# Decay attention then a two-layer block: own places for the first four jobs' inputs, and their transfers in program order

## The chip, the cores and the metric

The kernel runs on one core of a Trainium2 chip. Five engines work side by side, each through its own list of instructions in a fixed order: TensorE (PE in the profile, its weight loads PEld), VectorE (DVE), ScalarE (ACT), GpSimd (POOL) and SyncE (SP), which here only issues transfers. The metric is the device time of one launch in microseconds; lower is better. What is shown as a time is the median of three runs.

## The reference

For 8 batches and 8 heads, with a sequence S of 576 and head size 64, attention with a decay is computed: the scores are `q k^T / 8`, to which the difference of two running sums of `log(clip(f))` is added, with a causal mask, a softmax over the row, and the product with `v`. The result is laid out as 4608 tokens of 512 features, and goes through `g(x @ w_in) @ w_out` with a hidden size of 2048:

```python
cum = np.cumsum(np.log(np.clip(f, 0.0001, 1.0)), axis=-1)
scores = scale * np.matmul(q, k.transpose(0, 1, 3, 2)) + cum[..., :, None] - cum[..., None, :]
attn = softmax(where(causal, -1e9, scores))        # divided by (sum + 1e-9)
x = np.matmul(attn, v)                              # then to (tokens, heads * head size)
h = x @ w_in
g = where(h >= 1, h, where(h <= -1, 0, (h + 1) ** 2 / 4))
out = g @ w_out
```

The two weights come as 64-bit floats, so each block of a weight is 1 MB to be loaded, and has to be split into two 16-bit parts on the chip. `q`, `k`, `v` and `f` are 32-bit floats.

## The kernel before, in words

**Jobs.** Attention is done in jobs, each one pair of heads of one batch. Batch 0 is cut in two by rows of the score matrix: jobs 0 to 3 are its four head pairs for the first 256 rows, jobs 4 to 7 the same pairs for rows 256 to 575; from job 8 on a job is a head pair with all 576 rows. A job's rows are taken in blocks of 128. For a block PE makes the scores (L482); POOL makes the decay part from a broadcast row of sums, `ck`, and masks it (L488, L492); DVE adds both and finds the row's extreme (L571); ACT takes the exponential with its sum (L575). For the first five jobs ACT then makes a diagonal of the reciprocal sums (L502), PE turns the block with it (L513, L519), ACT copies it out (L524), and PE multiplies it with `v` (L544), from where ACT and DVE write the two 16-bit parts of `x` (L551, L552). Later jobs go another way (L589, L595, a transfer that transposes, L615).

**Inputs.** `load` (L330) brings `q` and `k` of a job into one of two buffers, `qk32`, by the job's parity; `early_prepare` (L375) turns them with PE (L388) and copies them out (L389). `load_decay` (L359) brings one head's decay row into one of three `ck` buffers, broadcast to all partitions; the sums themselves, `cum_d`, are written to memory by `decay_sums` (L150). `split_values` (L427) brings `v` of a job. `value_load` (L243) brings all of batch 0's `v` once more, in four parts, for its largest value (L256), from which a scale follows.

**Weights.** There are sixteen blocks, n = 0 to 15, of 1 MB each: an even n from `w_in`, an odd one from `w_out`. `weight_load` (L195) brings a block to a raw place: most lie in places of the result that are filled later, some in a buffer of `x` (table `RAW`). A place can be loaded again only when its last block was converted. `weight_split` converts two blocks at a time, here called a pair of blocks: DVE rearranges bits (L211, L214, L217), ACT sums squares (L221), PE and DVE make a scale (L131 to L140), ACT writes the high part (L225), POOL (L227, L228) and DVE (L230) the low one. `CONVERT` says how many pairs are done at each job, `LOADS` and `AHEAD` how far the loads may run ahead.

**The second part.** A unit of it is 256 tokens by 256 hidden features: PE (L657), ACT (L666, L667), DVE (L668), ACT (L670), DVE (L671), PE (L685). Units are put between the blocks of attention as soon as tokens and weights are there; those of `EARLY` begin with the first four pairs of weight blocks and the first 512 tokens.

**What sets the order.** The program is written as one sequence; a scheduler then gives each engine its list, moving instructions by its own estimate of when they can start. `in_order` pins an instruction: pinned instructions keep the order of the program. On the chip each engine goes strictly through its list. All transfers are issued by SP; each also waits until the one eight places ahead of it has landed. Before the change, the loads are not pinned.

## Time and profile before

| what | us |
|---|---|
| median of three runs (1118.39, 1119.46, 1121.65) | 1119.46 |
| the profiled execution | 1118.56 |
| its span | 1116.8 |
| PE busy in the span | 1017.8 |
| DVE busy in the span | 799.0 |
| ACT busy in the span | 790.0 |
| POOL busy in the span | 427.4 |

The span is the stretch from the first to the last instruction of the profiled execution; 1.8 us of its time lie outside. Times below count from the start of the span. In a row of the timeline stand the start, the time it took, the engine, the line, what is written from what, and how often; in brackets, how long the engine had been idle and what released it. "SPq" is the issue of a transfer, not its landing. A transfer's landing stands in the view of transfers, as a median from its issue. Line numbers are those of the kernel before; in the changed kernel the same code has other numbers (L153 became L158, L163 L172, L201 L210, L250 L265 or L267, L351 L362 or L378, L355 L382, L362 L389 or L399, L388 L428 or L433, L440 L480 or L499, L442 L501, L482 L541, L513 L572, L544 L603).

### The profile page before, as it was taken

The numbers are of one execution on the slowest core, as the hardware profiler recorded it, in microseconds if no ns is written. First come the engines' busy times: TensorE is split into PE (matmuls) and PEld (weight loads), VectorE is DVE, ScalarE is ACT, GpSimd is POOL, SyncE is SP. The second block draws the span as 40 slices with busy tenths as digits, with TensorE's granted clock in tenths as the row PEclk, the third lists the DMA queues.
The fourth block names the chain that finished last, engine by engine and source line by source line (L and its number), as shares of the span: only waits on it lengthen the run. The fifth ranks groups of instructions, "written<-read, shape, count | busy, mean of one in ns | idle before, by whom it ended". The sixth has DMA issues, their size and how long they took to land. (4 is left out here: it accounts for less than half of the span.)

```text
span 1116.8 us, 24410 instructions
## 1 busy us (share of the span) xinstructions
PE 1017.8 (91%) x8811; PEld 663.8 (59%) x8811; DVE 799.0 (72%) x2095; ACT 790.0 (71%) x1638; POOL 427.4 (38%) x679
## 2 busy tenths in 40 slices
PE   4647789667999999999999999999999999999998
PEld 3424455335566666666766666566666666677665
DVE  4785987887989888887667668888888787322222
ACT  3665887756877887788667768787878887444443
POOL 3486665634544543343223324344343442000000
PEclk9968889778999999999999999999999999999999
DMA  7957765575978657766653666775776462200000
GB/s 235 303 143 222 167 147 125 142 191 116 190 172 166 159 143 170 167 152 148 118 140 78 155 119 153 168 174 139 166 167 155 116 124 73 66 21 1 19 20 19
DMA packets 408281, 152.18 MB, mean 136 GB/s; under 512 B 383968, under 2 KB 384992, under 8 KB 408160
## 3 DMA queue, kind: packets, MB, share of 16 engines
q1 hardware_dynamic: 408160, 150.63, 57.6%
q8 instruction: 69, 1.13, 0.4%
q14 instruction: 52, 0.43, 0.1%
HBM read 75.64 MB, written 9.58 MB: 76 GB/s over the span
## 5 line engine op out<-in xcount | busy, mean ns | idle before, releaser
L657 PE MATMUL ph<-x,place 128*128 128x256 f16 (+3 forms) x4608 | 413.3, 248 | 6.4 <-DVE u L668 5.5
L685 PE MATMUL po<-place,g 128*128 128x512 f16 x1728 | 401.9, 382 | 12.4 <-ACT g L670 8.2
L657 PEld LDWEIGHTS <-place 128*128 128x128 f16 x4608 | 354.1, 99 | 66.3 <-issue 18.0
L685 PEld LDWEIGHTS <-g 128*128 128x128 f16 x1728 | 166.4, 99 | 192.0 <-ACT g L670 10.5
L488 POOL TENSOR_SCALAR sdr<-ck,nsig,cqs 128x128 f32<-128x128 f32 (+1 forms) x192 | 145.8, 763 | 149.2 <-DVE pr L595 137.3
L575 ACT ACTIVATE sdr<-sdr,nm 128x384 f32<-128x384 f32 (+1 forms) x248 | 137.4, 554 | 66.9 <-DVE nm L571 57.0
L668 DVE SCALAR_TENSOR_TENSOR u<-ph,z,u 128x512 f32<-128x512 f32 x128 | 95.8, 748 | 113.1 <-ACT u L667 112.5
L488 POOL TENSOR_SCALAR sd<-ck,nsig,cqs 64x576 f32<-64x576 f32 x48 | 60.0, 1250 | 248.7 <-ACT qs L414 109.3
L666 ACT ACTIVATE u<-ph,z 128x512 f32<-128x512 f32 x128 | 97.9, 765 | 78.4 <-PE ph L657 78.4
L482 PE MATMUL s<-qkT 64*64 64x512 f16 (+11 forms) x1056 | 119.6, 342 | 34.1 <-DVE nm L571 30.6
L595 DVE SCALAR_TENSOR_TENSOR pr<-sdr,rc,pr 128x384 f16<-128x384 f32 (+2 forms) x232 | 130.5, 596 | 21.6 <-ACT pr L589 20.4
L670 ACT ACTIVATE g<-u,z 128x512 f16<-128x512 f32 x128 | 91.9, 718 | 67.6 <-DVE u L668 67.3
L671 DVE SCALAR_TENSOR_TENSOR g<-u,z,g 128x512 f16<-128x512 f32 x128 | 96.7, 756 | 47.2 <-ACT g L670 46.5
L589 ACT ACTIVATE pr<-sdr,rc 128x384 f16<-128x384 f32 (+1 forms) x236 | 119.3, 556 | 12.1 <-DVE rc L586 5.3
L571 DVE CUSTOM_DVE_ANT_0 sdr<-s,sdr,nalpha 128x128 f32<-128x128 f32 (+1 forms) x192 | 99.0, 545 | 13.1 <-PE s L482 8.3
L492 POOL TENSOR_SCALAR_AFFINE_SELECT sdr<-sdr 128x128 f32<-128x128 f32 x248 | 93.9, 389 | 9.7
L667 ACT ACTIVATE u<-u 128x512 f32<-128x512 f32 x144 | 89.5, 622 | 2.0
L615 PE MATMUL s<-pT,vs 128*64 128x320 f16 (+3 forms) x1098 | 70.9, 282 | 4.7 <-DVE nm L571 4.7
L615 PEld LDWEIGHTS <-vs 128*64 128x64 f16 x1098 | 49.7, 112 | 27.3 <-issue 8.8
L488 POOL TENSOR_SCALAR sdr<-ck,cq 128x384 f32<-128x384 f32 (+3 forms) x56 | 39.9, 712 | 66.2 <-DVE pr L595 38.3
L482 PEld LDWEIGHTS <-qkT 64*128 64x128 f16 (+1 forms) x864 | 33.8, 99 | 51.3 <-issue 35.9
L414 ACT ACTIVATE qs<-qk,sc 128x640 f16<-128x640 f32 x48 | 37.0, 818 | 22.4 <-DVE sc L140 22.4
(154 smaller groups left out, 1013.8 us busy)
## 6 DMA issues: line engine op xcount, KB each, us to landing
ck<-cum_d SPq DMA_DIRECT2D x64, 288.0 KB, 3.8
out_dram<-ot SPq DMA_DIRECT2D x36, 256.0 KB, 2.1
qk<-in_k_dram SPq DMA_DIRECT2D x64, 128.0 KB, 2.7
vst<-in_v_dram SPq DMA_DIRECT2D x28, 288.0 KB, 3.3
v<-in_v_dram SPq DMA_DIRECT2D x62, 128.0 KB, 2.6
qk<-in_q_dram SPq DMA_DIRECT2D x56, 128.0 KB, 2.7
place<-in_moe_w_in_dram SPq DMA_DIRECT2D x6, 1024.0 KB, 7.2
place<-in_moe_w_out_dram SPq DMA_DIRECT2D x5, 1024.0 KB, 7.2
```

The lines of the kernel that those rows point to most:

```text
L482: nc.tensor.matmul(sds[h % len(sds)][1][p0:p1, c0:c1], lhsT=a[rows, q0 - w.s0:q0 - w.s0 + p1 - p0], rhs=b[rows, c0:c1], start=(i == 0), st ...
L488: nc.gpsimd.tensor_scalar(out=sd[p0:p1, 0:wid], in0=w.ck[h][p0:p1, 0:wid], scalar1=w.nsig if w.p < NQK else w.nsig[p0:p1], scalar2=w.cqs[p ...
L571: nc.vector.tensor_tensor_reduce(out=a, in0=sp[:, 0:wid], in1=a, scale=w.nalpha, scalar=BIG, op0=ALU.add, op1=ALU.min, accum_out=nm[:, i:i ...
L575: nc.scalar.activation(a, a, AF.Exp, bias=nm[:, i:i + 1], scale=-1.0, accum_out=sm[:, i:i + 1])
L589: nc.scalar.activation(pr[:, :, 0, i, :], a, AF.Copy, scale=rc[:, i:i + 1])
L595: nc.vector.scalar_tensor_tensor(out=pr[:, :, 1, i, :], in0=a, scalar=rc[:, i:i + 1], in1=pr[:, :, 0, i, :], op0=ALU.mult, op1=ALU.subtract,)
L615: nc.tensor.matmul(av[64 * h:64 * h + 64, at + s0:at + s1], lhsT=w.vs[:, vl, h, t, :], rhs=w.pT[:, t, pl, h, s0:s1], start=(t == 0 and pi ...
L657: nc.tensor.matmul(ph[:, fi, a0:a1], lhsT=wi[fb][:, wl, t, fi * P:(fi + 1) * P], rhs=xs[b][:, t, xl, s0:s0 + a1 - a0], start=(fi == 0 and ...
L666: nc.scalar.activation(u, h, AF.Relu, scale=z.u[:, i:i + 1], bias=z.h[:, i:i + 1])
L668: nc.vector.scalar_tensor_tensor(out=u, in0=h, scalar=z.t[:, i:i + 1], in1=u, op0=ALU.max, op1=ALU.min)
L671: nc.vector.scalar_tensor_tensor(out=g[:, 1], in0=u, scalar=z.r[:, i:i + 1], in1=g[:, 0], op0=ALU.mult, op1=ALU.subtract)
L685: nc.tensor.matmul(po[ch][i], lhsT=g[:, gl, fi * TC + i * P:fi * TC + (i + 1) * P], rhs=wo[fb][:, wl, fi, :], start=(first and fi == 0 and ...
```

## The change

For jobs 0 to 3, `load` puts `q` and `k` of each job in a part of its own in the `qk32` buffers (two jobs share one buffer, side by side), so the loads of jobs 2 and 3 don't wait until the ones of jobs 0 and 1 are used. A partition now holds two neighbouring rows of the sequence, so one transfer brings both heads of `q`, or of `k`, where two did before. The decay rows of both heads of such a job come in one transfer, into one of the four output tiles `ot`, which the second part uses only later. Two jobs also share one `v` buffer. Because rows now lie in pairs, `early_prepare` turns them with eight multiplications by the identity (64 columns each, one half of the output partitions for each head) where four transposes did it before. The `qk32` buffers are no longer cleared.

The transfers at the start are written in a new order, and `started` pins them, up to the loads issued in the step of job 4: the decay input first, then `q`, `k`, batch 0's values and `v` of jobs 0 and 1, the sums, the decay rows, and then by turns two weight blocks and a job's inputs. `LOADS` changes with it: six weight blocks are loaded before job 0.

```diff
-LOADS = {0: 3, 1: 6, 2: 8}
+LOADS = {0: 6, 1: 7, 2: 8}
...
+    def started(ins):
+        if start[0]:
+            in_order(ins)
...
-    for t in qk32 + [v32]:
-        nc.gpsimd.memset(t, 0.0)
+    nc.gpsimd.memset(v32, 0.0)
...
+        if ji < NPAIR:
+            n = 2 * 2 * D
+            for j, src in enumerate((q, k)):
+                at = (2 * (ji // 2) + j) * n
+                w.x32.append(flat[:, at:at + n])
+                started(nc.sync.dma_start(
+                    w.x32[j].rearrange("p (h e) -> p h e", h=2),
+                    src[w.b, h0:h0 + 2, 0:w.s1].rearrange("h (p n) d -> p h (n d)", p=P),
+                ))
+            return w
...
+    def load_first_decay(w):
+        bh = w.b * H + 2 * w.hp
+        ck = two.tile([P, DM], F32, name="ot", bufs=4)
+        ck = ck.rearrange("p (h s) -> p h s", h=2)
+        started(nc.sync.dma_start(
+            ck, cum_d[bh:bh + 2, 0:w.s1].rearrange("(o h) s -> o h s", o=1).broadcast_to([P, 2, w.s1])
+        ))
+        w.ck += [ck[:, 0], ck[:, 1]]
...
+            if w.p < NPAIR:
+                rows = w.x32[j].rearrange("p (h n d) -> p h n d", h=2, n=2)
+                cols = pt[:, 0:n].rearrange("c (p n) -> c n p", n=2)
+                for i in range(2):
+                    for h in range(2):
+                        nc.tensor.matmul(
+                            cols[64 * h:64 * h + 64, i], lhsT=rows[:, h, i], rhs=ident, start=True, stop=True
+                        )
...
+    decay_load()
     pairs = [load(0)]
+    value_load(0, 0)
+    value_load(0, 1)
+    pairs.append(load(1))
+    value_load(0, 2)
+    value_load(0, 3)
+    first_values(pairs[0])
     decay_sums()
-    pairs.append(load(1))
-    load_decay(pairs[0], 0)
-    load_decay(pairs[0], 1)
+    load_first_decay(pairs[0])
+    load_first_decay(pairs[1])
+    first_values(pairs[1])
+    load_weights(2)
+    for i in range(2, NPAIR):
+        pairs.append(load(i))
+        load_first_decay(pairs[i])
+        first_values(pairs[i])
+        load_weights(2 * i)
     prepare(pairs[0])
-    for i in range(NPAIR + 1):
-        value_step(0, i)
+    for i in range(NPAIR):
+        value_max(0, i)
     value_scale(0)
-    split_values(pairs[0])
-    pairs.append(load(2))
...
-                if r == w.r0 and p + 3 < njobs:
+                if r == w.r0 and NPAIR <= p + 3 < njobs:
...
+        start[0] = p < NPE
```

The scheduler's lists differ from the old ones up to about the tenth job, and are the same from there. Two places matter for what follows. The first is the start of PE's list. `qk_0` and `qk_1` are the two buffers of `q` and `k`, `s` the scores' place, `po` the product with `v`. Before:

```order
L482 MATMUL s<-qkT 128x128 x2
L482 MATMUL s<-qkT 128x256 x2
L120 MATMUL ph<-ident,m_162 1x128
L124 MATMUL ph<-top,ones 128x1
L388 MATMUL s<-ident,qk_0_98 128x128 x4
L482 MATMUL s<-qkT 128x128 x2
L482 MATMUL s<-qkT 128x256 x2
L513 MATMUL ph<-pr_112,sdr_101 128x128
...
L544 MATMUL po_337<-pT,vs 64x256 x2
```

and now:

```order
L541 MATMUL s<-qkT 128x128 x2
L127 MATMUL ph<-ident,m_184 1x128
L541 MATMUL s<-qkT 128x256 x2
L131 MATMUL ph<-top,ones 128x1
L572 MATMUL ph<-pr_110,sdr_101 128x128
...
L428 MATMUL s<-ident,qk_0_98 64x128 x8
L603 MATMUL po_337<-pT,vs 64x256 x2
L603 MATMUL po_337<-pT,vs 64x128 x2
L541 MATMUL s<-qkT 128x128 x2
L541 MATMUL s<-qkT 128x256 x2
```

The scores of job 1, the second pair of rows from L482 or L541, stood ahead of job 0's turning and its product with `v`; now they stand behind both, and behind job 2's eight new multiplications.

The second place is SP's list around the decay rows of job 5 (`ck_618` and `ck_695` before, `ck_614` and `ck_691` now) and the second set of weight blocks. Before:

```order
L362 DMA ck_505<-cum_d_88 128x576
L362 DMA ck_618<-cum_d_88 128x576
...
L362 DMA ck_695<-cum_d_88 128x576
...
L201 DMA place_90<-in_moe_w_out_dram 128x2x1024
...
L201 DMA place_90<-in_moe_w_in_dram 128x4x512
...
L201 DMA x_78<-in_moe_w_in_dram 128x4x512
L201 DMA place_90<-in_moe_w_in_dram 128x4x512
```

and now:

```order
L399 DMA ck_501<-cum_d_88 128x576
...
L210 DMA place_90<-in_moe_w_in_dram 128x4x512
L210 DMA place_90<-in_moe_w_out_dram 128x2x1024
L210 DMA x_78<-in_moe_w_in_dram 128x4x512
L210 DMA place_90<-in_moe_w_in_dram 128x4x512
L210 DMA x_80<-in_moe_w_out_dram 128x2x1024
L399 DMA ck_614<-cum_d_88 128x576
L378 DMA qk32_1_99<-in_q_dram 128x2x64 x2
...
L399 DMA ck_691<-cum_d_88 128x576
```

Job 5's decay rows stood ahead of the four weight blocks; now they stand behind five, the first of which waits for POOL to finish the third pair of weight blocks (L228), and the fourth for POOL to finish the fourth pair.

More of the change, by code (lines that the diff above doesn't have):

```diff
@@ L99 @@
     in_order = tc.keep_in_program_order
+    start = [True]
+    newest = [None]
+    def started(ins):
+        if start[0]:
+            in_order(ins)
     def even_pow2(dst, src):
@@ L148, with decay_load @@
     cq = const.tile([P, NT5, B * H], F32, name="cq")
+    def decay_load():
+        in_order(nc.sync.dma_start(early[0:B * H, 0:S], f.rearrange("b h s -> (b h) s")))
     def decay_sums():
@@ L152, in decay_sums @@
         nb = B * H
-        nc.sync.dma_start(fl[0:nb, 0:S], f.rearrange("b h s -> (b h) s"))
         nc.vector.tensor_scalar(
@@ L162, in decay_sums @@
         )
-        nc.sync.dma_start(cum_d, cum)
+        in_order(nc.sync.dma_start(cum_d, cum))
         pt = ps.tile([P, 1024], F32, name="s")
@@ L200, in weight_load @@
             src = w_out.bitcast(I32)[i * 2 * P:(i + 1) * 2 * P, :].rearrange("(t p) c -> p t c", p=P)
-        nc.sync.dma_start(raw(n).rearrange("p (t c) -> p t c", t=src.shape[1]), src)
+        ins = nc.sync.dma_start(raw(n).rearrange("p (t c) -> p t c", t=src.shape[1]), src)
+        started(ins)
+        newest[0] = ins.ins
     def weight_split(n0, n1):
@@ L241 @@
     vpart = [None]
+    vparts = []
     def value_load(b, i):
@@ L248, in value_load @@
             vpart[0] = stage[:, i * S:(i + 1) * S]
+            vparts.append(vpart[0])
         part = v[b, 2 * i:2 * i + 2].rearrange("h s d -> (h s d)").rearrange("(p n) -> p n", p=P)
-        nc.sync.dma_start(vpart[0], part)
+        if b == 1 and i == 0:
+            with tc.issue_after(newest[0]):
+                nc.sync.dma_start(vpart[0], part)
+        else:
+            started(nc.sync.dma_start(vpart[0], part))
     def value_max(b, i):
@@ L256, in value_max @@
         in_order(nc.vector.tensor_reduce(
-            out=vmax[b][:, i:i + 1], in_=vpart[0], axis=AX.X, op=ALU.max, apply_absolute_value=True
+            out=vmax[b][:, i:i + 1], in_=vpart[0] if b else vparts[i], axis=AX.X, op=ALU.max, apply_absolute_value=True
         ))
@@ L336, in load @@
         w.cuts = [(w.s0, w.s1)] if w.s1 - w.s0 <= 512 else [(0, 64), (64, S)]
+        w.ck = []
         h0 = 2 * w.hp
@@ L385, in early_prepare @@
             n = w.s1 - P * t0
-            for c0 in range(0, n, P):
+            if w.p < NPAIR:
+                rows = w.x32[j].rearrange("p (h n d) -> p h n d", h=2, n=2)
[5 more added lines that the diff above has]
+                        )
+            for c0 in range(0, n if w.p >= NPAIR else 0, P):
                 m = min(P, n - c0)
@@ L425, in prepare, with first_values @@
         w.terms = ((qh, kh), (ql, kh), (qh, kl))
+    def first_values(w):
+        h0 = 2 * w.hp
+        if w.p % 2 == 0:
+            t = two.tile([P, 2, 2, NT5, D], F16, name="vs")
+            pairs_v[0] = t.rearrange("p l h t d -> p (l h t d)").bitcast(F32)
+        n = 2 * 2 * D
+        w.vs = pairs_v[0][:, (w.p % 2) * n:(w.p % 2 + 1) * n].rearrange("p (h t d) -> p h t d", h=2, t=2)
+        for hh in range(2):
+            started(nc.sync.dma_start(w.vs[:, hh], v[w.b, h0 + hh, 0:w.s1, :].rearrange("(t p) d -> p t d", p=P)))
+    pairs_v = [None]
     def split_values(w):
+        if w.p < NPAIR:
+            return
         h0 = 2 * w.hp
@@ L439, in split_values @@
         for hh in range(2):
-            nc.sync.dma_start(dst[:, hh, 0:full, :], s_[hh, 0:P * full, :].rearrange("(t p) d -> p t d", p=P))
+            started(nc.sync.dma_start(dst[:, hh, 0:full, :], s_[hh, 0:P * full, :].rearrange("(t p) d -> p t d", p=P)))
         if w.r1 == NT5:
-            nc.sync.dma_start(dst[0:64, :, LAST, :], s_[:, FULL:S, :].rearrange("h p d -> p h d"))
+            started(nc.sync.dma_start(dst[0:64, :, LAST, :], s_[:, FULL:S, :].rearrange("h p d -> p h d")))
         if w.p < NPE:
```

12 lines of the change are left out of this document (6 added, 6 removed).

## The prediction

> **What bounds the kernel now.** I read the page first, then the table by stages, then the waits in the stages where PE has holes.
>
> ```profile
> span 1116.8 us, 24410 instructions
> PE 1017.8 (91%) x8811; PEld 663.8 (59%) x8811; DVE 799.0 (72%) x2095; ACT 790.0 (71%) x1638; POOL 427.4 (38%) x679
> ```
>
> ```profile
> core 0: us, PE busy (x) PEld busy (x) DVE busy (x) ACT busy (x) POOL busy (x), PEclk, DMA share, GB/s
> 0.00:12.00 12.00, 4.36 (x19) 2.84 (x21) 5.94 (x8) 4.02 (x7) 5.16 (x17) 1.00 0.67 179
> 12.00:28.10 16.10, 8.85 (x39) 5.57 (x37) 5.33 (x27) 6.84 (x22) 5.82 (x16) 1.00 0.87 274
> 28.10:83.40 55.30, 30.67 (x132) 20.00 (x132) 44.60 (x95) 37.62 (x86) 36.00 (x39) 0.84 0.75 223
> 83.40:111.50 28.10, 21.67 (x126) 13.55 (x122) 15.63 (x46) 15.85 (x31) 16.99 (x24) 0.89 0.80 223
> 111.50:280.00 168.50, 128.67 (x880) 77.35 (x882) 141.41 (x402) 123.11 (x259) 91.91 (x128) 0.85 0.65 149
> 280.00:1117.00 837.00, 823.62 (x7625) 544.45 (x7619) 586.06 (x1522) 602.55 (x1235) 271.53 (x457) 1.00 0.54 122
> ```
>
> From 280 us on PE is busy 823.6 of 837, so the end is set by when that stretch begins. Before it PE is busy only 194 of 280, and DVE is the fullest engine between 28 and 83 us (44.6 of 55.3) and after 111 us. The change acts before 111 us; behind that the lists soon are the same, and I let a microsecond won or lost at 111 us arrive whole at the end. I therefore follow DVE through three places: the start, the stretch to the fourth pair of weight blocks, and job 5.
>
> **The start: job 1 gains nothing.**
>
> ```profile
> 9.74 0.81 SPq L362 DMA_DIRECT2D ck<-cum_d  x2
> 13.51 1.42 POOL L488 TENSOR_SCALAR sdr<-ck,cq 128x128 f32<-128x128 f32 x3 [7.75 <-DMA ck<-cum_d]
> 18.53 1.65 PE L482 MATMUL s<-qkT 64*128 64x128 f32 x8 [0.45 <-ACT qkT L389]
> 20.11 2.93 PE L513 MATMUL ph<-pr,sdr 128*128 128x128 f32 x12
> 23.72 1.55 PE L544 MATMUL po<-pT,vs 128*64 128x256 f32 x8 [0.69 <-ACT pT L524]
> 26.28 1.44 POOL L488 TENSOR_SCALAR pr<-ck,cq 128x128 f32<-128x128 f32 x2 [6.69 <-DMA ck<-cum_d]
> 28.36 0.42 DVE L571 CUSTOM_DVE_ANT_0 pr<-s,pr 128x256 f32<-128x256 f32 x1
> 39.16 0.94 POOL L488 TENSOR_SCALAR sdr<-ck,cq 128x128 f32<-128x128 f32 x2 [6.55 <-DMA ck<-cum_d]
> ```
>
> Job 0's decay rows hang on the sums, whose chain is not shortened: 9.74 to 13.51 stays. Job 1's second decay row came at 26.28 and job 2's at 39.16, behind weight blocks; now they come before the first blocks, or early between them, so this wait goes. But job 1's scores, at 18.53 before, now stand behind job 0's turning (to 23.04), eight new multiplications and the product with `v`. The cost of the eight:
>
> ```profile
> L388 PE MATMUL s<-ident,qk 128*128 128x128 f32 x16 | 4.7, 437 | 3.8 <-DVE nm L571 3.5 <-ACT qkT L389 0.2
> L513 PE MATMUL ph<-pr,sdr 128*128 128x128 f32 x12 | 2.9, 434 | 0.0
> ```
>
> Four transposes of a job took 4 x 4.7/16 = 1.2 us. An ordinary 32-bit multiplication of 128 columns (L513, two records each) takes 2.9/6 = 0.48. The new ones alternate between halves of the output partitions as the product with `v` does; its eight records (four of 256 columns, four of 128) would take 4 x 0.48 + 4 x 0.24 = 2.9 one after the other and took 1.55, so halves overlap about twofold. Bounds: 1.2 (as transposes) to 3.9 (8 x 0.48, no overlap); I take 8 x 0.48/2 = 1.9, since L544 has their shape. So: 23.0 + 1.9 + 1.55 + 1.65 = 28.1 for the end of job 1's scores, and with the two last L571 (0.42 and 0.08 each) 29.1, where before the last ended at 28.36 + 0.42 = 28.8. **Cost 0.3 us**, in spite of the earlier input; between about 0 and 2.5.
>
> Here a rule of the Trainium skill weighs against the change: "TensorEngine Tiling (Array Packing)", section "Gotcha 2: Feature Incompatibilities", says that column tiling and the 32-bit transpose mode exclude each other, and "TensorE: Matmul & The Clock Gate", section "Terms", gives that mode a factor of four. By it the eight would take 8 x 4 x 0.29/2 = 4.7 us, and the start would cost 3.1 instead of 0.3. The rows of L513 show a factor of only 0.48/0.29 = 1.7, so I stay with 1.9, and keep the other as a rival.
>
> **28 to 83 us: what the early rows bring.**
>
> ```profile
> DVE sdr L571 <- POOL sdr L492: 5.4, 3, 2.6
> DVE mp L132 <- PE ph L131: 2.6, 2, 1.9
> DVE pr L571 <- POOL pr L492: 2.1, 3, 1.2
> ```
>
> ```profile
> L448 DVE SCALAR_TENSOR_TENSOR vs<-v,sv,vs 128x640 f16<-128x640 f32 x1 | 0.9, 869 | 0.0
> ```
>
> DVE idles 55.3 - 44.6 = 10.7 us here; 5.4 + 2.1 = 7.5 of it wait for POOL's decay parts, and POOL in turn waited for decay rows. Those rows now lie ready: job 3's stand ahead of the fifth weight block. I keep 1.5 of the 7.5, because L571 will now and then wait for scores that PE makes later, and take 6.0. L448 of job 5 leaves this stretch (0.9). With the 0.3 above the fourth pair's scale comes 6.0 + 0.9 - 0.3 = **6.6 us earlier**. Bounds: 0 (PE and ACT take the place of POOL in every wait) and 10.7 (no idle left).
>
> **Job 5: a new wait.**
>
> ```profile
> 80.90 2.12 POOL L228 TENSOR_TENSOR place<-place 128x1024 f16<-128x1024 f32 x1
> 83.05 0.37 SPq L201 DMA_DIRECT2D place<-in_moe_w_in_dram  x1
> 83.29 0.17 DVE L140 RECIPROCAL sw<-mp 128x2 f32<-128x2 f32 x1
> 85.83 1.28 DVE L230 SCALAR_TENSOR_TENSOR place<-x,sw,place 128x1024 f16<-128x1024 f32 x1 [0.85 <-ACT place L225]
> 89.20 1.28 POOL L488 TENSOR_SCALAR sdr<-ck,cq 128x384 f32<-128x384 f32 x2
> 90.88 0.56 DVE L571 CUSTOM_DVE_ANT_0 sdr<-s,sdr 128x384 f32<-128x384 f32 x1 [3.76 <-POOL sdr L492]
> ```
>
> ```profile
> 18.50:25.50 7.00, 6.05 (x28) 4.33 (x28) 0.86 (x5) 3.54 (x12) 1.02 (x3) 1.00 1.06 388
> ```
>
> ```profile
> x<-in_f_dram SPq DMA_DIRECT2D x1, 144.0 KB, 2.8
> ```
>
> Job 5's rows lay ready at 89.20. Now five weight blocks stand ahead of them in SP's list, and the first waits for the L228 that ended at 83.02, earlier by the same 6.6: issue at 83.05 - 6.6 = 76.4. A transfer alone in the queue lands after 2.8 us, 0.4 of it for its own bytes; full, the queue moves 388 GB/s, so 1024 KB (1.05 MB) take 2.7 us and a decay row of 288 KB 0.8. The row lands at 76.4 + 2.4 + 5 x 2.7 + 0.8 = 93.1; the first L571 follows 90.88 - 89.20 = 1.7 later, at 94.8: **3.9 us later than before**. Queued behind it are all of POOL's and DVE's job 5, and its scores' places. Bounds: from no wait, if the blocks were issued earlier, to the whole 16.7 us after 83.05.
>
> **To job 6: what is not paid twice.**
>
> ```profile
> 99.16 0.78 ACT L666 ACTIVATE u<-ph,early_z 128x512 f32<-128x512 f32 x1 [0.67 <-PE ph L657]
> 101.78 0.62 ACT L667 ACTIVATE u<-u 128x512 f32<-128x512 f32 x1
> 103.36 0.75 DVE L668 SCALAR_TENSOR_TENSOR u<-ph,early_z,u 128x512 f32<-128x512 f32 x1
> 104.14 0.72 ACT L670 ACTIVATE g<-u,early_z 128x512 f16<-128x512 f32 x1 [0.29 <-DVE u L668]
> 105.28 0.74 DVE L671 SCALAR_TENSOR_TENSOR g<-u,early_z,g 128x512 f16<-128x512 f32 x1
> 109.03 0.75 DVE L256 TENSOR_REDUCE m<-vst 128x1 f32<-128x576 f32 x1 [3.01 <-DMA vst<-in_v_dram]
> 111.56 0.55 DVE L571 CUSTOM_DVE_ANT_0 sdr<-s,sdr 128x384 f32<-128x384 f32 x1
> ```
>
> The first unit of the second part now stands ahead of job 5 on DVE and ACT, so it is done inside the new wait: 0.75 + 0.74 on DVE and 0.78 + 0.62 + 0.72 on ACT, which held up job 5's high parts, are gone from here. The second L256, with its wait of 3.01, now stands behind job 6's first two L571. L448 comes in (0.9). Sum: 1.5 + 2.1 + 3.0 - 0.9 = **5.7 us shorter**. Bounds: 3.6 (ACT's share is hidden anyway) and 8.3 (all idle of DVE from 90.88: 20.7 less 12.4 busy). What of L211, L214 and L256 now stands behind job 6 is only moved, and counted neither way.
>
> **Sum:** 3.9 - 5.7 = -1.8 us at job 6, so 1116.8 for the profiled execution of 1118.56, and, the median of the runs lying 0.9 above it, 1117.7; I say 1117.5. With g for what the first 83 us bring, the sum is 4.8 - g (6.6 here); g from 0 to 10.7 and the last step from 3.6 to 8.3 give +6.9 to -8.5, or 1126 to 1111. The pinned transfers themselves, the cleared buffers that go (POOL, ahead of 13.51) and the larger `q` and `k` transfers cost nothing: the wait for job 0's sums covers them; without it, they would be worth under 1 us.
>
> **The rivals.**
> *The wait does not form.* If the blocks ahead of job 5's rows land by the time POOL is free, job 5 follows the unit: L230 ends at 87.1 - 6.6 = 80.5, the unit takes 6.7 (3.04 of PE and the five operations above), job 5 starts at 87.2, 3.7 before 90.88, and with the 5.7 the gain is 9.4: 1110. For it: SP may issue early, as only two of the five blocks wait for late work. Against: the first waits for L228 of the third pair, and the order is fixed.
> *Slower: the wait is paid in full.* If job 1's late scores drag jobs 2 to 4 along, so that g stays near 0, job 5 starts at 83.05 + 16.7 + 1.7 = 101.4, 10.6 late, and 5.7 or 3.6 come back: +5 to +7, 1124.5 to 1126.5. For it: PE's list is now strictly behind job 0, and DVE's weight operations already fill 28 to 83. It decides from g under about 1.4, given the 0.3% that a measurement of this kernel can tell from no change (3.4 us).
> *The eight multiplications are dear,* as the skill's rule would have them: 2.8 more at the start, g 3.8, sum +1.0: 1120.5. For it: no row shows such a multiplication; against: L513.
>
> **How the numbers follow.** Forecast (1113 to 1121) 0.50: faster 0.18, same 0.30, slower 0.02. No wait 0.20: faster. Full wait 0.22: slower. Dear multiplications 0.08: same 0.06, slower 0.02. So faster 0.38, same 0.36, slower 0.26. The range leaves out little of either rival: 1108 to 1126; the forecast's own is 1113 to 1121.
>
> **What would show it.** Job 1's L571 ends near 29; POOL no longer waits for a decay row in jobs 1 to 3; L140 of the fourth pair comes near 77 instead of 83.3; POOL then waits for a decay row of job 5 for several us, and DVE's next L571 starts near 95; job 6's first L571 stands near 108 with 2.7 us of moved DVE work behind it. The prediction is wrong if L140 comes at 83 or later, if POOL's wait for job 5 is missing, or if the distance between 111 and 280 us changes by more than 3 us.

## The result, and the profile after

The changed kernel takes 1130.53 us (median of six runs, 1128.09 to 1132.57), the kernel before 1119.11 in six runs beside it: a ratio of 1.010, 95% interval 1.008 to 1.012. It is **slower by 1.0%**, 11.4 us, where 1117.5 was forecast, with 1108 to 1126 as the range. The profiled execution is the longest of the six, 1132.57 us, and its span is 1130.8, 14.0 more than before.

The page of the changed kernel:

```profile
span 1130.8 us, 24467 instructions
PE 1035.5 (92%) x8859; PEld 674.9 (60%) x8859; DVE 796.4 (70%) x2095; ACT 791.2 (70%) x1638; POOL 421.6 (37%) x677
```

Lines of its table by stages, with the stretch from job 6's first step on DVE to job 8's as the last row:

```profile
core 0: us, PE busy (x) PEld busy (x) DVE busy (x) ACT busy (x) POOL busy (x), PEclk, DMA share, GB/s
28.10:83.40 55.30, 39.04 (x169) 26.42 (x170) 48.06 (x110) 40.05 (x92) 32.24 (x29) 0.60 0.56 166
83.40:111.50 28.10, 19.21 (x91) 10.96 (x90) 11.94 (x26) 13.88 (x27) 14.15 (x24) 0.74 0.75 246
...
280.00:1130.00 850.00, 839.48 (x7716) 553.90 (x7714) 595.09 (x1559) 611.27 (x1251) 279.02 (x468) 0.99 0.54 121
113.90:161.30 47.40, 32.83 (x202) 20.30 (x198) 34.53 (x85) 33.67 (x62) 27.55 (x33) 0.74 0.75 155
```

DVE does the same 2095 instructions. From 28 to 83 us it now gets more done (48.06 against 44.60 us), from 83 to 111 less (11.94 against 15.63). From 280 us on PE has 839.5 us of work left instead of 823.6, and does it with the same 11 to 13 us of idle time: the loss is made ahead of 280, as a late start of PE's full stretch.

When a job begins, seen by DVE's first operation on its scores (L571 before, L630 now), says where. Positive differences are late:

| first operation of | before | after | difference |
|---|---|---|---|
| job 4 | 68.21 | 56.32 | -11.9 |
| job 5 | 90.88 | 98.29 | +7.4 |
| job 6 | 111.56 | 113.91 | +2.4 |
| job 8 | 151.09 | 161.29 | +10.2 |
| job 9 | 177.51 | 187.93 | +10.4 |
| job 15 | 345.19 | 358.85 | +13.7 |
| end of the span | 1116.8 | 1130.8 | +14.0 |

Job 5 is late, as forecast, and job 6 has won most of that back, as forecast. The surprise is job 8 in the table: 7.8 us go between jobs 6 and 8, and they stay lost. Another 3.3 go between jobs 9 and 15.

**Job 5.** From the timeline of the changed kernel, SP, POOL and DVE one after the other:

```profile
78.25 0.38 SPq L210 DMA_DIRECT2D place<-in_moe_w_in_dram  x1
84.77 0.57 SPq L210 DMA_DIRECT2D x<-in_moe_w_out_dram  x1
85.39 0.72 SPq L399 DMA_DIRECT2D ck<-cum_d  x1
95.68 1.38 POOL L547 TENSOR_SCALAR sdr<-ck,cq 128x384 f32<-128x384 f32 x2 [11.35 <-DMA ck<-cum_d]
78.48 0.17 DVE L147 RECIPROCAL sw<-mp 128x2 f32<-128x2 f32 x1
93.52 0.75 DVE L730 SCALAR_TENSOR_TENSOR g<-u,early_z,g 128x512 f16<-128x512 f32 x1 [0.79 <-ACT g L729]
98.29 0.56 DVE L630 CUSTOM_DVE_ANT_0 sdr<-s,sdr 128x384 f32<-128x384 f32 x1 [4.02 <-POOL sdr L551]
```

Job 5's first decay row is issued behind five weight blocks, and POOL waits 11.35 us for it.

**Job 8.** The same kernel around the sixth pair of weight blocks. L663 are two transfers that transpose the last block of job 6, L652 is the low part of that block, which they wait for, and L399 at 141.06 the second decay row of job 8. L239 is the low part of the fifth pair, L232 are the squares and L139 the norms of the sixth; L273 at 117.96 is the second L256 of the prediction:

```profile
136.99 2.54 SPq L663 DMA_TRANSPOSE pT<-pr  x2
139.62 1.39 SPq L382 DMA_DIRECT2D qk<-in_k_dram  x1
141.06 0.59 SPq L399 DMA_DIRECT2D ck<-cum_d  x1
135.56 1.40 POOL L652 TENSOR_TENSOR pr<-sd,pr 128x640 f16<-128x640 f32 x1
137.06 1.06 POOL L547 TENSOR_SCALAR sd<-ck,cq 64x576 f32<-64x576 f32 x1
145.29 0.75 POOL L547 TENSOR_SCALAR sd<-ck,cq 64x576 f32<-64x576 f32 x1 [6.01 <-ACT sdr L634]
147.75 2.12 POOL L239 TENSOR_TENSOR place<-place 128x1024 f16<-128x1024 f32 x1
149.90 1.11 ACT L232 ACTIVATE place<-place 128x1024 f16<-128x1024 f32 x1 [2.23 <-POOL place L239]
117.96 0.75 DVE L273 TENSOR_REDUCE m<-vst 128x1 f32<-128x576 f32 x1 [3.01 <-DMA vst<-in_v_dram]
152.88 0.16 DVE L139 TENSOR_SCALAR mp<-ph 128x2 f32<-128x2 f32 x1 [6.48 <-PE ph L138]
159.66 0.28 DVE L129 TENSOR_REDUCE top<-ph 1x1 f32<-1x128 f32 x1 [2.47 <-PE ph L127]
161.29 0.29 DVE L630 CUSTOM_DVE_ANT_0 sdr<-s,sdr 128x128 f32<-128x128 f32 x1
```

SP can issue the two transposes only when POOL has made job 6's low part (L652 ends at 136.96), and the row of job 8 stands behind them. It lands at 145.20, and POOL, idle for 6.01 us, starts at 145.29. The view names ACT's L634, which ends at 145.20 too, as the releaser; but L547 reads the row and nothing that L634 writes, so I take it for a wait for the row, and the runs below bear that out. POOL's low part of the fifth pair comes behind, ACT's squares write into the place that it reads, and DVE stands 6.48 us at L139 and then 2.47 at L129.

In the kernel before, the same row was issued ahead of the same two transposes (L604 there), and POOL had it in time:

```profile
126.03 0.35 SPq L362 DMA_DIRECT2D ck<-cum_d  x1
130.92 2.53 SPq L604 DMA_TRANSPOSE pT<-pr  x2
130.75 1.90 POOL L488 TENSOR_SCALAR sd<-ck,cq 64x576 f32<-64x576 f32 x2
111.50:151.10 39.60, 29.53 (x235) 20.57 (x235) 36.60 (x92) 33.71 (x63) 24.94 (x28) 0.91 0.66 154
```

Between its first steps of jobs 6 and 8 DVE was idle 39.6 - 36.6 = 3.0 us there; now it is 47.40 - 34.53 = 12.9. Of the 9.9 more, 3.0 are the wait at L273, which stood ahead of job 6 before; the waits of 6.48 and 2.47 are new. What made the waits at jobs 5 and 8, and whether they are the loss, is what the runs had to tell.

### The profile page after: what moved, and what is told of

It reads as the page before. It is cut to its first block, busy times and chain, and to the rows that moved or that the text cites. A ratio compares the mean times of both kernels' runs of the same rounds, so it can differ in the third digit from the quotient of the medians.

```text
span 1130.8 us, 24467 instructions
## 1 busy us (share of the span) xinstructions
PE 1035.5 (92%) x8859; PEld 674.9 (60%) x8859; DVE 796.4 (70%) x2095; ACT 791.2 (70%) x1638; POOL 421.6 (37%) x677
## 5 line engine op out<-in xcount | busy, mean ns | idle before, releaser
L716 PE MATMUL ph<-x,place 128*128 128x256 f16 (+3 forms) x4608 | 418.7, 250 | 3.6 <-DVE u L727 3.2
L547 POOL TENSOR_SCALAR sdr<-ck,nsig,cqs 128x128 f32<-128x128 f32 (+1 forms) x192 | 144.6, 756 | 147.5 <-DVE pr L654 132.8
L634 ACT ACTIVATE sdr<-sdr,nm 128x384 f32<-128x384 f32 (+1 forms) x248 | 137.4, 554 | 64.9 <-DVE nm L630 55.8
L547 POOL TENSOR_SCALAR sd<-ck,nsig,cqs 64x576 f32<-64x576 f32 x48 | 59.2, 1234 | 253.7 <-ACT qs L459 111.2
L541 PE MATMUL s<-qkT 64*64 64x512 f16 (+11 forms) x1056 | 123.1, 349 | 18.8 <-DVE nm L630 12.9
L630 DVE CUSTOM_DVE_ANT_0 sdr<-s,sdr,nalpha 128x128 f32<-128x128 f32 (+1 forms) x192 | 99.2, 545 | 14.3 <-PE s L541 9.2
L674 PEld LDWEIGHTS <-vs 128*64 128x64 f16 x1098 | 50.0, 112 | 29.4 <-issue 11.7
L541 PEld LDWEIGHTS <-qkT 64*128 64x128 f16 (+1 forms) x864 | 33.7, 99 | 51.1 <-issue 34.7
L547 POOL TENSOR_SCALAR sdr<-ck,cq 128x384 f32<-128x384 f32 (+3 forms) x48 | 38.3, 798 | 55.7 <-DVE pr L654 33.9
```

The source lines that it names most:

```text
L541: nc.tensor.matmul(sds[h % len(sds)][1][p0:p1, c0:c1], lhsT=a[rows, q0 - w.s0:q0 - w.s0 + p1 - p0], rhs=b[rows, c0:c1], start=(i == 0), st ...
L547: nc.gpsimd.tensor_scalar(out=sd[p0:p1, 0:wid], in0=w.ck[h][p0:p1, 0:wid], scalar1=w.nsig if w.p < NQK else w.nsig[p0:p1], scalar2=w.cqs[p ...
L630: nc.vector.tensor_tensor_reduce(out=a, in0=sp[:, 0:wid], in1=a, scale=w.nalpha, scalar=BIG, op0=ALU.add, op1=ALU.min, accum_out=nm[:, i:i ...
L634: nc.scalar.activation(a, a, AF.Exp, bias=nm[:, i:i + 1], scale=-1.0, accum_out=sm[:, i:i + 1])
L674: nc.tensor.matmul(av[64 * h:64 * h + 64, at + s0:at + s1], lhsT=w.vs[:, vl, h, t, :], rhs=w.pT[:, t, pl, h, s0:s1], start=(t == 0 and pi ...
L716: nc.tensor.matmul(ph[:, fi, a0:a1], lhsT=wi[fb][:, wl, t, fi * P:(fi + 1) * P], rhs=xs[b][:, t, xl, s0:s0 + a1 - a0], start=(fi == 0 and ...
```

## The experiments

Ratios are to the kernel before on the same chip, with their 95% intervals. "Late" counts against the kernel before.

### Which part of the change

Four runs take one part away, or put one part into the kernel before. In the first, only the decay rows of jobs from 5 on lose their pin (the scheduler may issue them when it likes, and it makes the lists behind them anew):

```diff
-        started(nc.sync.dma_start(
+        (started if w.p <= NPAIR else id)(nc.sync.dma_start(
             ck[:, 0:w.s1], cum_d[bh:bh + 1, 0:w.s1].broadcast_to([P, w.s1])
```

> The changed kernel with one pin lifted: the decay rows of job 5 (and of later jobs) are no longer held in program order, so that SP issues both rows of job 5 ahead of the five weight blocks. Theory W (the loss is the wait of job 5 for its decay rows): POOL's wait of 11.3 us for a decay row near 95 us is gone, DVE's first L630 of job 5 comes at or before 90 instead of 98.3, job 6's first near 107 instead of 113.9, and the time falls by 7 to 14 us, to 1116 to 1124. Theory O (the loss is made behind 111 us, by another order of the work of jobs 6 to 8, whatever comes before): job 5 comes earlier as well, but the stretch from job 6's first L630 to job 9's first stays near the 74.0 us of the changed kernel (66.0 in the kernel before), and the time stays above 1124. Theory S (the start is dearer: eight multiplications and job 1's scores late): the time stays within 2 us of the changed kernel, 1128 to 1133.

In the second no transfer is pinned but the decay input and the store of the sums; the new places stay:

```diff
-        if start[0]:
+        if False:
             in_order(ins)
```

> The changed kernel with no load pinned from the first weight block on (only the decay input and the store of the sums stay pinned); places, row pairs and the count of blocks stay. Theory W: job 5's rows come ahead of the five weight blocks again, as in the kernel before, and the time is that of the run with one pin lifted, 1116 to 1124. Theory O: the stretch from job 6's first L630 to job 9's first stays near 74 us unless the order of jobs 6 to 8 is by chance that of the kernel before; above 1124. Theory S: 1128 to 1133, since the row pairs and PE's order at the start remain.

In the third, one edit to the kernel before: job 5's rows are issued behind the eleventh weight block (`newest` holds the loads of the blocks).

```diff
...
+        with (tc.issue_after(newest[10]) if w.p == 5 else contextlib.nullcontext()):
+            nc.sync.dma_start(ck[:, 0:w.s1], cum_d[bh:bh + 1, 0:w.s1].broadcast_to([P, w.s1]))
```

> The kernel before, with the two decay rows of job 5 issued behind the last of the four weight blocks that wait for the third and fourth pair; nothing else is edited. Theory W: job 5's first L571 waits for its row until about 97 to 99 instead of 90.9, and the time rises by 5 to 12 us, to 1124 to 1131. Theory O: the wait costs less than 3 us by job 6, and what the time then does depends on the order behind it; 1117 to 1123 if the stretch from job 6's first L571 to job 9's stays near 66 us. Theory S: no more than 3 us, 1119 to 1122.

In the fourth, `q` and `k` come one head per transfer again, and four transposes turn them:

```diff
...
-            if w.p < NPAIR:
+            if False:
...
-            for c0 in range(0, n if w.p >= NPAIR else 0, P):
+            for c0 in range(0, n, P):
```

> The changed kernel without the row pairs: q and k of the first four jobs come with one head per transfer, rows in blocks of 128, and four transposes turn them as before; places, pins and the order of the transfers stay. Theory S: job 1's last L630 near 29 comes 1 us or more earlier, the clock granted to PE between 28 and 83 us goes from 0.60 back towards the 0.84 of the kernel before, and the time falls by 4 us or more, to 1126 or less. Theories W and O: the start changes by less than 1 us and job 5's wait stays near 11 us, so 1127 to 1133; four more issues for each job on SP cost at most 2 us.

| | time, us | ratio | job 5 | job 8 | job 9 |
|---|---|---|---|---|---|
| rows of jobs from 5 on free | 1117.68 | 0.999 (0.998 to 1.000) | 86.09 | 148.75 | 176.00 |
| nothing pinned | 1124.02 | 1.004 (1.002 to 1.005) | 96.10 | 163.20 | 183.28 |
| before, rows of job 5 late | 1132.03 | 1.012 (1.010 to 1.013) | 101.10 | 155.58 | 190.52 |
| no neighbouring rows | 1128.58 | 1.008 (1.006 to 1.010) | 101.05 | 163.49 | 190.18 |

Freeing a few rows takes the whole loss away, and putting job 5's rows behind the blocks into the kernel before makes one of 13 us, more than even theory W gave it. So the places of the inputs and the eight multiplications are innocent (theory S falls with the fourth run), and the decay rows' place on SP is what costs. The third run has more in it than its edit: the scheduler moved job 8's second row as well, and issued it at 142.05, behind two transposes at 138.13, so POOL waits for it there too:

```profile
145.80 1.36 POOL L488 TENSOR_SCALAR sd<-ck,cq 64x576 f32<-64x576 f32 x1 [4.45 <-DMA ck<-cum_d]
```

The second run lies between the theories, at an edge: without these pins 5 us of the loss stay. They aren't a wait for the rows, as both rows of job 5 have landed by 57.94 and job 8's second stands ahead of the transposes (132.17 and 136.03). The last L147 ahead of job 5 comes at 84.79 there, against 78.48 in the changed kernel; what makes it late wasn't followed. How a wait of 7 us at job 5, of which 5 come back by job 6, makes 11, none of the four says.

### Is it the pairs of weight blocks?

After job 6 DVE waits at the sixth pair of weight blocks, and what it waits for are squares that ACT writes into a place which POOL still reads. Four runs ask whether the pairs are the loss. The fifth and the sixth pair are converted one job earlier each:

```diff
-CONVERT = {1: 1, 2: 1, 3: 2, 5: 1, 6: 1, 9: 1, 10: 2}
+CONVERT = {1: 1, 2: 1, 3: 2, 4: 1, 5: 1, 9: 1, 10: 2}
```

in the changed kernel, in the one with free rows, and in the kernel before; and in another run the squares are written over words of their own block that nothing reads any more:

```diff
-            nc.scalar.activation(place[:, n, 1], words[-1], AF.Square, accum_out=m2[:, n - n0:n - n0 + 1])
+            nc.scalar.activation(low.bitcast(F32), words[-1], AF.Square, accum_out=m2[:, n - n0:n - n0 + 1])
```

> The changed kernel with the fifth and sixth pair of weight blocks converted one job earlier (at jobs 4 and 5 in the program, where it was 5 and 6); pins and the wait of job 5 stay. In the runs so far the end followed two things alike, and this run parts them: DVE's last step of the sixth pair (148.9 us in the kernel before, 162.7 in the changed one, 149.2 with the rows free, 166.7 with late rows) and job 9's first L630 (177.5, 187.9, 176.0, 190.5). Theory P (the end hangs on the fifth and sixth pair, of which the units wait): the conversion of the fifth pair fills DVE's idle stretch from 82 to 98 us, the last step of the sixth comes near 135, earlier than in the kernel before, and the time falls by 10 us or more, to 1119 or less. Theory J (the end hangs on when the attention jobs get through): job 5 and job 6 start no earlier than in the changed kernel, and the time gains only what of DVE's idle time is filled, 4 to 8 us: 1122 to 1127.

> The changed kernel with ACT's squares of a weight block (a by-product that nobody reads) written over the dead low words of the block itself, where they went into a part of the place in which the fifth pair's raw block still lies. In the changed kernel the sixth pair's squares stood ready from 139.3 us and ran at 149.9, when POOL's L239 of the fifth pair had ended. If that dependency is what held them: they run before 143, DVE's 6.5 us of waiting for the sixth pair's sums go, and its last step comes 4 to 8 us earlier than 162.7. By theory P the time then falls by 4 to 8 us, to 1122 to 1127; by theory J by no more than 3, to 1127 to 1131. If ACT's own list held them, nothing moves: 1128 to 1133.

> Both edits that worked against a cause: job 5's decay rows free of the pin, and the fifth and sixth pair of weight blocks converted one job earlier. Theory P: the last step of the sixth pair comes near 135 against 149.2 with the rows free alone, and the time is 1104 to 1113. Theory J: conversion takes DVE's time from jobs 5 and 6, whose lead of 12 us at job 6 shrinks; 1114 to 1120.

> The kernel before with the fifth and sixth pair of weight blocks converted one job earlier; nothing else. Theory P: the last step of the sixth pair comes 8 us or more earlier than 148.9 and the time falls by more than 3.4 us, below 1115. Theory J: DVE has the same work in another order, and the time stays within 3.4 us of the kernel before, 1115 to 1122.

Measured: 1122.83 (ratio 1.005, 1.003 to 1.007) for the changed kernel with the early pairs, 1117.33 (1.000, 0.998 to 1.001) with free rows besides, 1119.72 (1.002, 1.000 to 1.003) for the kernel before with it, and 1131.51 (1.012, 1.009 to 1.015) for the squares apart. In that one the sixth pair no longer waits for POOL, but POOL still waits for the row:

```profile
146.63 0.76 POOL L547 TENSOR_SCALAR sd<-ck,cq 64x576 f32<-64x576 f32 x1 [6.63 <-DMA ck<-cum_d]
145.95 0.15 DVE L139 TENSOR_SCALAR mp<-ph 128x2 f32<-128x2 f32 x1
```

(changed kernel with the squares apart, POOL and DVE). The wait of 6.48 at L139 is gone, and the time is what it was: up to job 9's first step DVE is idle 55.3 us instead of 62.8, but has done 131.2 us of work instead of 125.1. So the chain through the squares is there, and taking it away brings nothing: theory P, which lays the loss to the pairs, falls. (Theory J gave 1127 to 1131 for this run, which is 0.5 us above.) The other three have the times that theory J gave. Early pairs bring half of the loss back in the changed kernel, by the ratios, and nothing where the rows are free.

### Order of the lists, or the rows?

In each of these kernels the scheduler also made other lists for PE, DVE, ACT and POOL. To part that from the rows, the lists were held: instructions of one engine are chained, with no wait on the chip, in the order of a table taken from another kernel.

```diff
+    for e, chain in ORDER.items():
+        row = [by[e][n] for n in chain]
+        for a, b in zip(row, row[1:]):
+            tc.add_manual_dep(
+                b, a.name, mybir.DependencyInfo(mybir.DependencyClass.NoSync, mybir.DependencyReason.DATA), reason="order"
+            )
```

Here `by` holds an engine's instructions and `ORDER` the table; only the table differs between the kernels. Five were run, each with PE, DVE, ACT and POOL held and SP left to the scheduler: the kernel before in the changed kernel's order from job 5 to job 10; the kernel with free rows in the order of before over the same stretch; the changed kernel in that order; the kernel with free rows in the order of before to the end; and the kernel with free rows in the changed kernel's own order, from the first unit to the end.

> The kernel before, in which from job 5 on, up to about job 10, the lists of PE, DVE, ACT and POOL are held (by pins without waits) in the order that the changed kernel has there; the start, the places and SP's transfers stay those of the kernel before, so job 5's rows are there in time. Theory O (a good part of the loss is the order of the lists behind job 5, which the scheduler made anew): DVE's idle time from job 6's first L571 to job 8's first rises from 3.0 us to 8 or more, and the time is 1122 to 1130. Theory W (the order doesn't matter, all of the loss is the wait for the rows): 1116 to 1121.

> The changed kernel with job 5's decay rows free of the pin, and from job 5 on, up to about job 10, the lists of PE, DVE, ACT and POOL held in the order of the kernel before. Theory O: the lead at job 5 (86 to 88 us against 90.9) passes through, DVE idles no more than 5 us from job 6's first L630 to job 8's first (8.1 with the rows free and the scheduler's own order), and the time is 1112 to 1116, faster than the kernel before. Theory W: as with the rows free alone, 1116 to 1119.

> The changed kernel, with all its pins and so with the wait of job 5 for its rows, and from job 5 on the lists of PE, DVE, ACT and POOL held in the order of the kernel before. Theory O: job 5 begins 7 us late as in the changed kernel, the first unit no longer fills a part of the wait, and the lateness passes through unchanged: job 9's first L630 7 to 9 us later than in the kernel before, 1125 to 1128. Theory W: the order changes nothing, 1128 to 1133.

> As the run with the rows free and the order of the kernel before, but with the lists of PE, DVE, ACT and POOL held in that order from job 5 to the end of the program, where they were held to about job 10 only. In that run a lead of 3.8 us at job 5 and 4.0 at job 9 shrank to 0.8 at job 15, and from DVE's 600th instruction on its order was again another one than in the kernel before. Theory L (a lead passes through where the order stays): 3 to 4 us ahead at job 15 too, and 1112 to 1116, faster than the kernel before. Theory N (the later part, bound by PE, takes back a lead whatever the order): 1117 to 1120, no change against the kernel before.

> The changed kernel with job 5's decay rows free of the pin, and the lists of PE, DVE, ACT and POOL held in exactly the changed kernel's own order from the first unit on. So the wait for the rows goes and nothing else moves. Theory W (the wait for the rows is what makes the loss): job 5's first L630 comes before 91, and the time is 1117 to 1121. Theory O (the order would hold job 5 anyway: DVE has the first unit ahead of it, which ends near 94): job 5 begins at 94 to 96 instead of 98.3, the stretch from job 6 to job 9 stays near 74 us, and the time falls by no more than 4 us, to 1126 to 1130.

| | time, us | ratio | job 5 | job 8 | job 9 |
|---|---|---|---|---|---|
| before, in the order of after | 1129.68 | 1.009 (1.006 to 1.012) | 99.76 | 160.36 | 186.98 |
| rows free, order of before to job 10 | 1120.68 | 1.002 (1.001 to 1.004) | 87.06 | 150.83 | 173.50 |
| after, in the order of before | 1133.87 | 1.013 (1.011 to 1.016) | 101.07 | 165.84 | 188.50 |
| rows free, order of before to the end | 1115.87 | 0.998 (0.997 to 1.000) | 87.37 | 150.51 | 173.07 |
| rows free, order of after | 1117.85 | 1.000 (0.999 to 1.002) | 96.85 | 153.53 | 179.69 |

The last row says that the order of the four engines' lists isn't to blame by itself: with the changed kernel's own lists from the first unit on, and the rows free, the loss is gone, though job 5 comes just 1.4 us earlier than in the changed kernel (96.85 against 98.29). That is the time that theory W gave, with job 5 nearly as late as theory O had it (94 to 96). (Ahead of the first unit, and on SP, the scheduler was free here.) The first row seems to say the contrary. Both have the same four lists from the first unit on, and are level on DVE at 145.3 us; then the kernel before in this order loses 6.8 us up to job 8's first step. What differs is SP: with free rows, job 8's second row was issued at 132.96, ahead of the two transposes (135.17); in the other at 140.14, behind them (136.84).

```profile
143.77 1.00 POOL L488 TENSOR_SCALAR sd<-ck,cq 64x576 f32<-64x576 f32 x1 [4.62 <-DMA ck<-cum_d]
151.95 0.16 DVE L132 TENSOR_SCALAR mp<-ph 128x2 f32<-128x2 f32 x1 [5.30 <-PE ph L131]
```

(The kernel before in the order of after, POOL and DVE.) That is the picture of the changed kernel at job 8. The third kernel came out slower than either theory gave, with job 5's delay of 10.2 us passed on whole to job 9 (+11.0): in the order of before nothing makes it up. The fourth row, 1115.87 us, is **faster than both kernels**, though only just: by 0.2% against the kernel before, with an upper end of the interval at 0.9997; the lead of 4.4 us at job 9 is still 3.7 at the end of its span, 1113.1 (2.0 in the medians). The second, outside the range of either theory, loses a like lead between job 10 and the end, where the scheduler was free.

### The rows alone

The last four hold all five lists, SP's too, in the changed kernel's order and move only decay rows on SP: job 8's second row ahead of the two transposes, job 5's first row ahead of the five blocks, both rows of job 5, and all three. In the traces of these four, all lists are those of the changed kernel from start to end but for the rows that were moved. The transposes are job 6's: the trace has job 7's first step on DVE at 135.12, 1.9 us before them; the expectation of the first of these runs calls them job 7's.

```diff
 L660 DMA_TRANSPOSE pT<-pr_1043 128x16x128
+L399 DMA ck<-cum_d 128x576
 L663 DMA_TRANSPOSE pT<-pr_1138 128x10x64 x2
 L382 DMA qk_0_98<-in_k_dram 64x2x64
-L399 DMA ck<-cum_d 128x576
```

```diff
+L399 DMA ck<-cum_d 128x576 x2
 L210 DMA place<-in_moe_w_in_dram 128x4x512
...
 L210 DMA x<-in_moe_w_out_dram 128x2x1024
-L399 DMA ck<-cum_d 128x576
...
-L399 DMA ck<-cum_d 128x576
```

> All five engines' lists are held in the changed kernel's own order through the first ten jobs; only the second decay row of job 8 moves on SP, ahead of the two transposes of job 7 behind which it was issued at 141.06. Theory Q (decay rows that queue on SP behind transfers which wait for other work make the loss, at job 5 and again at job 8): POOL's wait of 6.0 us before job 8's decay part is gone or under 2, the sixth pair's step on DVE (L139) waits under 3 us instead of 6.5, job 9's first step comes 4 to 7 us earlier than in the changed kernel, and the time is 1122 to 1127. Rival R (the loss is job 5's alone, and the wait at job 8 only takes the place of another): 1128 to 1132.

> The lists are held in the changed kernel's order; only job 5's first decay row moves on SP, ahead of the five weight blocks; its second row stays behind them. Theory Q: the first step of job 5 comes to 88 to 93 us, but its second head's row still lands about 97 to 100, so job 6 gains little: 1127 to 1131. Rival R (job 5's first row was the loss): 1118 to 1124.

> The lists are held; both decay rows of job 5 move on SP ahead of the five weight blocks, nothing else. Theory Q: job 5 starts at 88 to 95, its loss goes but job 8's row still stands behind the transposes: 1120 to 1126. Rival R: the whole loss goes, 1116 to 1120. Rival T (neither row matters by itself; what helped where SP was left to the scheduler was the place of the other transfers): above 1127.

> Both moves together, the lists otherwise held in the changed kernel's order. Theory Q: 1116 to 1121, the time of the kernel before, with no wait of POOL above 3 us for a decay row at jobs 5 and 8. Rival R: the same as with job 5's rows alone, within 1.5 us. Rival T: above 1125.

In the last column stands DVE's idle time between its first steps of jobs 6 and 8:

| moved ahead | time, us | ratio | job 5 | job 6 | job 8 | job 9 | DVE idle |
|---|---|---|---|---|---|---|---|
| nothing (the changed kernel) | 1130.53 | 1.010 (1.008 to 1.012) | 98.29 | 113.91 | 161.29 | 187.93 | 12.9 |
| first row of job 5 | 1131.95 | 1.012 (1.010 to 1.014) | 93.87 | 113.08 | 160.51 | 186.90 | 12.4 |
| both rows of job 5 | 1126.11 | 1.006 (1.004 to 1.008) | 95.10 | 111.35 | 158.96 | 185.57 | 12.9 |
| second row of job 8 | 1123.55 | 1.005 (1.004 to 1.006) | 97.75 | 113.36 | 154.97 | 181.20 | 6.3 |
| all three | 1119.40 | 1.002 (1.000 to 1.003) | 94.97 | 111.98 | 153.39 | 179.53 | 6.2 |

With the row of job 8 ahead, SP, POOL and DVE:

```profile
133.81 0.53 SPq L399 DMA_DIRECT2D ck<-cum_d  x1
136.59 3.60 SPq L663 DMA_TRANSPOSE pT<-pr  x2
138.99 1.74 POOL L547 TENSOR_SCALAR sd<-ck,cq 64x576 f32<-64x576 f32 x1
150.07 0.16 DVE L139 TENSOR_SCALAR mp<-ph 128x2 f32<-128x2 f32 x1 [2.30 <-PE ph L138]
154.97 0.29 DVE L630 CUSTOM_DVE_ANT_0 sdr<-s,sdr 128x128 f32<-128x128 f32 x1
```

POOL's wait of 6.01 is gone, the one at L139 fell from 6.48 to 2.30, the one of 2.47 at L129 is gone too, job 9 comes 6.7 us earlier, and this one place of one transfer of 288 KB gives 7.0 us of the 11.4 back. It gives 6.7 once more where job 5's rows are ahead already. Both rows of job 5 give 4.4. Together they give 11.1, nearly the sum. (By the ratios, which take the chips' difference out, it is 5.8, 4.3 and 9.5 us of 11.2; the interval for job 5's rows alone, 1.004 to 1.008, just meets that of the changed kernel.) That the holding itself gains nothing is seen in the run with job 5's first row, which has the changed kernel's time. That is what theory Q said, with job 5's rows at the very edge of its range (1126.1 for 1120 to 1126); the theory that job 5's rows are the whole loss, and the one that no row matters, fall. The first row of job 5 alone brings nothing (1131.95, 1 us above Q's 1127 to 1131), since the second head's row still lands behind the blocks, at 97.87:

```profile
97.96 1.37 POOL L547 TENSOR_SCALAR sdr<-ck,cq 128x384 f32<-128x384 f32 x2 [9.92 <-DMA ck<-cum_d]
100.58 0.56 DVE L630 CUSTOM_DVE_ANT_0 sdr<-s,sdr 128x384 f32<-128x384 f32 x1 [5.54 <-POOL sdr L551]
```

(first row of job 5 ahead, POOL and DVE). And with all three ahead, job 5 no longer waits for a row:

```profile
92.77 0.75 DVE L727 SCALAR_TENSOR_TENSOR u<-ph,early_z,u 128x512 f32<-128x512 f32 x1 [8.78 <-ACT u L726]
94.31 0.75 DVE L730 SCALAR_TENSOR_TENSOR g<-u,early_z,g 128x512 f16<-128x512 f32 x1 [0.79 <-ACT g L729]
94.97 0.55 DVE L630 CUSTOM_DVE_ANT_0 sdr<-s,sdr 128x384 f32<-128x384 f32 x1
```

It starts right behind the first unit, on which DVE waits 8.78 us. So of the wait at job 5 only 98.29 - 94.97 = 3.3 us is the row's own (5 at most, as this run is 1.6 us later from the fourth pair's L147 on, at 80.11); without it the unit, which now stands ahead of job 5 on DVE, takes its place. This is where job 4's lead of 11.9 us ends even with the rows in time.

## Why the prediction was wrong

**The start: right.** PE, DVE and POOL of the changed kernel:

```profile
23.82 1.98 PE L428 MATMUL s<-ident,qk 128*64 128x128 f32 x16
26.52 0.93 PE L541 MATMUL s<-qkT 64*128 64x128 f32 x8
28.94 0.42 DVE L630 CUSTOM_DVE_ANT_0 pr<-s,pr 128x256 f32<-128x256 f32 x1
24.08 1.98 POOL L547 TENSOR_SCALAR sdr<-ot,cq 128x128 f32<-128x128 f32 x4 [3.53 <-DMA ot<-cum_d]
```

The eight multiplications took 1.98 us (1.9 forecast), and job 1's last operation of DVE ends at 29.4 (29.1). The rule that the Trainium skill gives in "TensorEngine Tiling (Array Packing)", "Gotcha 2: Feature Incompatibilities", with the factor of "TensorE: Matmul & The Clock Gate", "Terms", made an estimate of 4.7 of it; this trace doesn't agree, with 1.98, and the measurement decides. With that the rival of dear multiplications falls, and the run with four transposes again, no faster than 1128.58, says the same. That POOL would wait for no row in jobs 1 to 3 was wrong for job 2 (the 3.53 us above; its row landed at 23.91), which cost nothing there: DVE's first step of job 2 stands at 35.06.

**28 to 83 us: the mechanism right, the size too large.** L147 of the fourth pair stands at 78.48, against 83.29: g is 4.8, not 6.6, and DVE's idle time fell from 10.7 to 7.2. None of its waits for POOL is left there; waits for ACT took part of their place (the longest 1.6 us, at L637). So the rival in which g stays near 0 falls too; it had the right sign for another reason.

**Job 5: the wait is there, larger than sized.** First block issued at 78.25 (76.4 forecast), the row landed at 95.50 (93.1), first operation at 98.29 (94.8): 7.4 us late, not 3.9. So the rival in which no wait forms falls. Of the 3.5 us between them 1.9 are the smaller g; from issue to landing it was 17.25 against 16.7; and 2.8 us from landing to DVE against 1.7.

**To job 6: right.** 98.29 to 113.91 are 15.6 us, 5.1 less than the 20.7 before (5.7 forecast). With the two sizes above the sum was 7.4 - 5.1 = +2.3 instead of -1.8, and the time would have been some 1121, inside the range. (The bound of 8.3 took DVE's work from 90.88 to job 6 as 12.4 us; the view gives 12.85, so 7.8.)

**The step that failed** is the one behind: "what of L211, L214 and L256 now stands behind job 6 is only moved, and counted neither way", with "I let a microsecond won or lost at 111 us arrive whole at the end". The distance from job 6 to job 9, taken as fixed, grew by 8.0 us: +2.4 became +10.4. Up to job 8 it is 7.8: DVE works 2.1 us less there and is idle 9.9 us more. Two things made that idle time. The smaller is the wait of 3.0 at the second L256: the sum took it off ahead of job 6 as won and counted nothing behind, where it is back with 3.01 (L273 at 117.96). With it the sum is some +5.3, or 1124, still inside the range; no run takes this wait away by itself, so what it costs at the end is not shown. The larger is a transfer that the prediction never looked at: the second decay row of job 8, which in the changed kernel's list on SP stands behind two transposes that wait for job 6's last block. The prediction gave that very argument, a row behind transfers that wait for other work, at job 5 and stopped there. Moving this row alone gives 7.0 us back; moving job 5's rows 4.4, of which 2.4 are seen at job 9 and the rest further behind, where it wasn't traced. The prediction's last sentence named the sign to look for, a stretch from 111 to 280 us longer by over 3 us; it gave it no price and no chance.

Four things stay open. Why the scheduler places the row of job 8 behind the transposes wasn't tried: it isn't pinned itself. Where the kernel before with late rows of job 5 loses the 8.5 us between jobs 8 (+4.5) and 9 (+13.0) wasn't followed. Nor were the 3.3 us that the profiled execution of the changed kernel loses between jobs 9 and 15. And the lead of some runs at job 9 (4.0 us with free rows in the order of before) is lost or kept behind job 10 with the order there, by a place that wasn't looked for.

## What to carry to other kernels

In this kernel, a list of transfers issued by one engine was a queue in which each entry waits for its own inputs: whatever a small, early-needed transfer stands behind, it also waits for what those transfers wait for (job 8's row went out at 141.06 us behind two transposes, and at 133.81 ahead of them). When a change moves the order of such a list, walk the whole of it, in the order as built, for every small transfer that stands behind one waiting for late work, and price each by what its reader has queued behind itself. A late job is no safe end for a sum: compare the lists up to where the order is the same again, not up to the first place where the clock looks level.
